# Retention and a mixture of experts on one core: where gating, weight splits and transposed rows stand in the engines' queues

## The chip, the cores and the metric

The kernel runs on one core of a Trainium2 chip. A core has five engines with a queue of instructions each: TensorE (PE; its weight loads are listed as PEld), VectorE (DVE), ScalarE (ACT), GpSimd (POOL) and SyncE (SP), which issues most of the transfers. Each queue is worked off in its order, and engines wait for one another by semaphores. The metric is the time of one execution on the device in microseconds (us), as the median of several.

## What is computed

Two steps stand one behind the other. The first is retention: attention without a softmax, causal, with a decay for each head. The second is a mixture of eight experts, in which each row goes to one expert.

```python
scores = scale * np.matmul(q, k.transpose(0, 1, 3, 2))     # q, k, v: 8 x 8 heads x 576 x 64
Dmat = np.where(rel >= 0, gamma[:, None, None] ** rel[None, :, :], 0.0)
x = np.matmul(scores * Dmat[None], v)                      # then as rows: x is 4608 x 512

logits = x @ w_gate                                        # 512 x 8
e_idx = np.argmax(logits, axis=1)
gate_w = softmax(logits)[np.arange(N), e_idx]
eom = 1.0 / (1.0 + np.exp(-(x @ w_output_gate)))
for e in range(E):                                         # 8 experts
    mask = e_idx == e
    h = np.maximum(x[mask] @ w1[e], 0.0)                   # 512 x 1024
    ye = h @ w2[e]                                         # 1024 x 512
    out[mask] = gate_w[mask, None] * eom[mask, e, None] * ye
```

Everything is float32. The host only rearranges arrays and adds tables of constants (decays, masks, row numbers).

## The kernel before

**Retention.** The 4608 rows are 36 tiles of 128. A loop over g = 0 ... 35 (L494) works them off with a running state for each head, so that a tile needs its own scores and the state before it. In the loop's code stand, in this order: `load` (the pack of tile g+4: q and k transposed, v as it is), `prep` (GpSimd scales v to vp), `scores(g+1)` (TensorE; VectorE masks them from PSUM into S_sb, two instructions), `k_rows(g+1)` (TensorE transposes k, ScalarE copies it to kn), `xnat(g-1)` (TensorE turns the finished tile xT back into rows and, in the same matmuls, forms the gating logits; ScalarE copies the rows to xgrp, VectorE copies the logits to lg in two instructions), `outT(g)` (TensorE applies state and scores; VectorE scales the result into xT), and `update(g)` (TensorE adds to the state; ScalarE copies it to stT). Nine tiles are two sequences of 576 rows: with c = g modulo 9, tile c = 8 updates no state, tile c = 0 reads none, and c = 4 holds the seam of two sequences.

Inside the blocks called `manual_schedule` the order of the code is the order of each engine's queue. So what is written ahead of `outT` stands ahead of xT on VectorE, and TensorE's `xnat` of the next round waits for that xT.

**Gating.** Every GT = 4 tiles, `gate1` (L371) finds the expert of each of 512 rows (13 small instructions on VectorE and two exponentials on ScalarE), `gate2` counts rows by matmuls with 0/1 matrices, `gate3a` and `gate3b` (VectorE) make the slot number and the weight of each row. Then `scatter_x` on GpSimd writes the rows into a table xs in device memory, 4608 slots for each expert; its calls lie in a list, `todo`, from which each tile takes one or two. After group 5 (tile 26) `gate3b` also makes the slots that are filled up with zeros.

**Experts.** Each expert has room for 616 rows here: part 0 with 360 rows (tiles t = 0, 1, 2) and part 1 with 256 (t = 3, 4); rows beyond that go through a loop at the end (L666). Each operand is split into an upper part, rounded to float32r, and a lower part, the difference; a product takes three matmuls (hi x hi, hi x lo, lo x hi). `mm1(e, part, fb)` makes one 128-row block of h in 12 matmuls into one of four PSUM buffers h_ps; ScalarE writes relu(h_ps) as hh (L244), VectorE the rest as hl (L245). `mm2(e, t)` makes a tile of y in 24 matmuls into one of two buffers y_ps; ScalarE scales it, GpSimd scatters it to the output (L264). For each expert the loop at L625 runs fb = 0 ... 7 with both parts, then t = 0 ... 4.

The weights come in eight pieces an expert (w1 and w2, four each, 512 KB a piece) through three staging buffers st: `start_w` issues the load, `hi_w` makes the upper half on ScalarE (L137, two instructions), `lo_w` the lower half on VectorE (L142, two instructions); `load_w` (L144) does all three with both halves on VectorE (L146, L147). The pieces of expert 0 are spread over the retention stage by the table `wsched`: for each piece the tiles at which load, `hi_w` and `lo_w` come. The rows of expert e+1 are loaded during the first half of expert e (`load_x`) and transposed during its second half by `transp` (L210): from expert 1 on VectorE transposes (L224), ScalarE casts the upper part xh (L226), VectorE subtracts to xl (L227). For expert 0 TensorE transposes (L221), at tiles 34 and 35.

Of the kernel before, what the change touches and what calls it, by code (L numbers as in the profile page):

```python
# [10 lines left out]
F32 = mybir.dt.float32  # L11
# [36 lines left out]
def tile_retention_moe(  # L48
# [95 lines left out]
    def load_w(which, e, fp):  # L144
        st, hi, lo = start_w(which, e, fp)
        V.tensor_copy(hi, st)  # L146
        V.tensor_tensor(out=lo, in0=st, in1=hi.bitcast(F32), op=ALU.subtract)  # L147

# [60 lines left out]

    def transp(e, t):  # L210
        part, n = (0, TA * P) if t < TA else (1, CAP - CA)
        t0 = t if part == 0 else t - TA
        if (e, part) not in XT:
            pl = pools[f"xt{part}"]
            XT[e, part] = (pl.tile([P, KB, n], F32R, name=f"xh{part}"), pl.tile([P, KB, n], F32R, name=f"xl{part}"))
        m = ROWS[t] if e == 0 else P
        hi, lo = (a[:, :, P * t0:P * t0 + m] for a in XT[e, part])
        if e == 0:
            src = pools["ps_x"].tile([P, KB, P], F32, name=pools["x_ps"])[:, :, 0:m]
            for k in range(KB):  # L220
                T.transpose(src[:, k, :], XG[e, t][0:m, k:DM:KB], ident[0:m, 0:m])  # L221
        else:
            src = pools["xq"].tile([P, KB, P], F32, name="x_t", bufs=2)
            V.transpose(out=src.rearrange("p k (u j) -> p u k j", u=4),  # L224
                        in_=XG[e, t].rearrange("p u (i k) -> p u k i", k=KB))
        A.copy(out=hi, in_=src)  # L226
        V.tensor_tensor(out=lo, in0=src, in1=hi.bitcast(F32), op=ALU.subtract)  # L227

# [141 lines left out]

    def gate1(n):  # L371
        L = gt["lg"]
# [11 lines left out]
        oh = sm.tile([P, GT, E], BF16, name="oh")  # L384
        V.tensor_tensor(out=oh, in0=fst, in1=bc(m2), op=ALU.is_equal)
        c1 = sm.tile([P, GT, E], BF16, name="c1")
        if n == 0:
# [83 lines left out]
    for n in (512, 512, 256):  # L471
        T.matmul(warm[:, 0:n], lhsT=zx[:, 0:P], rhs=zx[:, 0:n], start=True, stop=True)
    prep(0)

    wsched = {(1, 0): (6, 10, 11), (1, 1): (10, 14, 15), (1, 2): (15, 18, 19), (1, 3): (18, 22, 23),
              (2, 0): (25, 28, 29), (2, 1): (28, 31, 31), (2, 2): (30, 33, 33), (2, 3): (34, 36, 36)}
    wparts = {}
# [13 lines left out]
    with tc.manual_schedule():  # L491
        S_next = scores(0)
        k_rows(0)
        for g in range(NTILE):  # L494
# [12 lines left out]
            if g + 1 < NTILE:  # L507
                prep(g + 1)
                S_next = scores(g + 1)
                if "sl" in gt:  # L510
                    gate3b()
                k_rows(g + 1)
            for _ in range(1 if g < GT * SNAP + 6 else 2):
                if todo:
                    G.memset(gap, 0.0)
                    todo.pop(0)()
            if g >= NTILE - 2:
                transp(0, g - NTILE + 2)
            if g > 0:
                xnat(g - 1)  # L520
            outT(g, S_sb, prev)
            update(g)
            if g == NTILE - 1:
                transp(0, 2)
            if g % GT == 0 and g > 0:
                gate1(g // GT - 1)
            weights(g)
    psctx.close()
# [5 lines left out]
    xnat(NTILE - 1)  # L534
    gate1(NTILE // GT - 1)
    p1ctx.close()
# [88 lines left out]
    for e in range(E):  # L625
        nx = e + 1 < E
        for fb in range(FB):
# [14 lines left out]
            elif nx:  # L642
                if fb < CT:
                    load_x(e + 1, fb)
                if fb in (5, 6):
                    load_idx(e + 1, fb - 5)
                if fb % 2 == 1:
                    load_w(1, e + 1, fb // 2)
            if fb == (7 if e else 4) and e + 2 < E:
                fill_slots(e + 2)  # L650
        if e == E - 1:
            overflow_table()
        for t in range(CT):
            if e > 0 or t >= TA:
                for u in (t,) if e else range(3) if t == TA else range(3, CT):
                    if nx:
                        transp(e + 1, u)
                mm2(e, t)
# [98 lines left out]
```

## Time and profile before

| | |
|---|---|
| time, median of 3 | 637.74 us (635.58 to 639.58) |
| the profiled execution | 639.73 us, of which the span from first to last instruction is 637.9 us |
| VectorE busy | 353.1 us in 748 instructions |
| ScalarE busy | 173.3 us in 387 instructions |
| mean granted TensorE clock | 0.995 of full speed |
| stages in this profile | retention to about 182 us, expert 0 to about 240 us, then about 55 us for each further expert |

A row of a profile gives the line of the kernel, the engine, the operation and its tiles as out<-in. In a timeline two numbers stand ahead: the start from the span's beginning and the duration in us; "xN" is the number of instructions merged into the row, and in brackets stands how long the engine had been idle before it and what ended that. In a list of waits the three numbers are the total in us, how often, and the longest. Matmuls overlap, so that one lasts longer than the distance from its start to the next one's.

### The profile page before, as it was taken

The page shows a single profiled execution, that of the slowest core. Times are in us where ns is not written, and L with a number is a line of the kernel's source. Part 1 is how long each engine was busy: PE and PEld are TensorE (multiplying, and loading weights), DVE is VectorE, ACT ScalarE, POOL GpSimd, SP SyncE. Part 2 cuts the span into 40 slices and gives each one's busy share as a digit, 9 for nine tenths or more (in the row PEclk, how much of TensorE's full clock was granted, in tenths as well). Part 3 has the DMA queues.
Part 4 walks back from the last instruction along what each step waited for, and adds up shares of the span by engine and source line. Part 5 has one row for each costly group of instructions (what it writes and reads, how often), then busy time and mean ns, then how long its engine had stood idle before and what let it go on. Part 6 is the DMA issues. An engine that isn't in the chain of part 4 may idle for free. (4 is left out here: it accounts for less than half of the span.)

```text
span 637.9 us, 12795 instructions
## 1 busy us (share of the span) xinstructions
PE 620.4 (97%) x5135; PEld 550.1 (86%) x5135; DVE 353.1 (55%) x748; ACT 173.3 (27%) x387; POOL 166.0 (26%) x229
## 2 busy tenths in 40 slices
PE   8999999999989998999999999999999999999995
PEld 6888888888879888978997997898799789879974
DVE  4576887767743266751862475186257528625420
ACT  2333434333431333222222222222222122222210
POOL 2243445454227315012301401230150110010011
PEclk9999999999999998999999999999999999999999
DMA  9867697786314654741733364173345407311001
GB/s 323 250 237 264 221 313 231 240 278 216 115 69 163 185 157 140 200 126 53 211 91 109 101 195 132 41 205 91 113 129 167 132 31 221 110 47 49 0 34 43
DMA packets 54746, 96.24 MB, mean 151 GB/s; under 512 B 14640, under 2 KB 35505, under 8 KB 54684
## 3 DMA queue, kind: packets, MB, share of 16 engines
q1 hardware_dynamic: 44972, 72.99, 37.7%
q0 software_dynamic: 9280, 21.36, 9.2%
q8 instruction: 41, 0.67, 0.4%
q10 hardware_dynamic: 432, 1.05, 0.4%
q14 instruction: 21, 0.17, 0.1%
HBM read 74.02 MB, written 30.64 MB: 164 GB/s over the span
## 5 line engine op out<-in xcount | busy, mean ns | idle before, releaser
L240 PE MATMUL h_ps<-xh,w1h 128*128 128x360 f32 (+1 forms) x512 | 157.0, 307 | 6.0 <-ACT xh L226 3.9
L240 PE MATMUL h_ps<-xl,w1h 128*128 128x360 f32 (+1 forms) x512 | 156.7, 306 | 0.5 <-DVE xl L227 0.5
L240 PE MATMUL h_ps<-xh,w1l 128*128 128x360 f32 (+1 forms) x512 | 156.5, 306 | 0.0
L264 POOL DMA_INDIRECT out_dram<-y,idx x40 | 40.4, 1009 | 340.4 <-ACT y L263 312.6
L258 PE MATMUL y_ps<-w2h,hh 128*128 128x512 f32 (+1 forms) x320 | 125.8, 393 | 0.0
L258 PE MATMUL y_ps<-w2h,hl 128*128 128x512 f32 (+1 forms) x320 | 125.3, 391 | 0.0
L258 PE MATMUL y_ps<-w2l,hh 128*128 128x512 f32 (+1 forms) x320 | 125.2, 391 | 0.0
L245 DVE SCALAR_TENSOR_TENSOR hl<-h_ps,hh 128x360 fp32r<-128x360 f32 (+1 forms) x128 | 58.3, 474 | 98.1 <-ACT hh L244 92.6
L240 PEld LDWEIGHTS h_ps<-xh,w1h 128*128 128x128 f32 x512 | 97.4, 190 | 7.4 <-ACT xh L226 4.4
L240 PEld LDWEIGHTS h_ps<-xl,w1h 128*128 128x128 f32 x512 | 97.4, 190 | 1.7 <-DVE xl L227 1.0
L244 ACT ACTIVATE hh<-h_ps 128x360 fp32r<-128x360 f32 (+1 forms) x128 | 54.4, 428 | 160.6 <-PE h_ps L240 150.8
L240 PEld LDWEIGHTS h_ps<-xh,w1l 128*128 128x128 f32 x512 | 97.2, 190 | 0.0
L258 PEld LDWEIGHTS y_ps<-w2h,hl 128*128 128x128 f32 (+1 forms) x320 | 58.8, 184 | 15.0
L258 PEld LDWEIGHTS y_ps<-w2l,hh 128*128 128x128 f32 (+1 forms) x320 | 58.8, 184 | 14.2
L258 PEld LDWEIGHTS y_ps<-w2h,hh 128*128 128x128 f32 (+1 forms) x320 | 58.8, 184 | 14.2
L227 DVE TENSOR_TENSOR xl<-x_t,xh 128x512 fp32r<-128x512 f32 x35 | 24.2, 693 | 80.3 <-ACT xh L226 78.2
L263 ACT ACTIVATE y<-y_ps,idx 128x512 f32<-128x512 f32 (+1 forms) x40 | 27.5, 688 | 148.2 <-issue 77.2
L330 DVE TENSOR_TENSOR S_sb<-sc,cmat_sb 128x512 f32<-128x512 f32 x72 | 46.1, 682 | 17.8 <-PE sc L324 15.8
L313 POOL TENSOR_TENSOR vp<-pk,gk_sb 128x512 f32<-128x512 f32 x36 | 37.4, 1040 | 67.2 <-PE st_ps L344 44.3
L188 POOL DMA_INDIRECT xs<-xgrp,sli x36 | 37.1, 1031 | 49.8 <-issue 37.1
L188 POOL DMA_INDIRECT xs<-zx,fill x40 | 46.6, 1165 | 9.4 <-issue 9.4
L324 PE MATMUL sc<-pk 64*128 64x128 f32 x576 | 45.1, 288 | 0.8 <-DVE S_sb L330 0.4
(119 smaller groups left out, 676.0 us busy)
## 6 DMA issues: line engine op xcount, KB each, us to landing
st<-in_w_dram SPq DMA_DIRECT2D x64, 512.0 KB
pk<-in_pack_dram SPq DMA_DIRECT2D x32, 768.0 KB
x_q<-xs SPq DMA_DIRECT2D x140, 64.0 KB
gq_sb<-in_gq_dram SPq DMA_DIRECT2D x5, 256.0 KB
pk<-in_pack_dram SPq DMA_DIRECT2D x4, 256.0 KB
pk<-in_pack_dram SPq DMA_DIRECT2D x2, 512.0 KB
x_g<-xs SPq DMA_DIRECT2D x4, 256.0 KB
xs<-zx,fill POOLq DMA_INDIRECT x40
```

What stands on the lines that cost most here:

```text
L188: i = G.indirect_dma_start(out=xs, out_offset=bass.IndirectOffsetOnAxis(ap=at, axis=0), in_=x, in_offset=None, **({} if bound is None else ...
L227: V.tensor_tensor(out=lo, in0=src, in1=hi.bitcast(F32), op=ALU.subtract)
L240: i = T.matmul(ps, lhsT=a[:, k, :], rhs=b[:, k, 0:n], start=(j == 0), stop=(j == 3 * KB - 1))
L244: A.activation(out=hh, in_=ps, func=AF.Relu)
L245: V.scalar_tensor_tensor(out=hl, in0=ps, scalar=0.0, in1=hh.bitcast(F32), op0=ALU.max, op1=ALU.subtract)
L258: i = T.matmul(ps, lhsT=a[:, n], rhs=b, start=(j == 0), stop=(j == 3 * FB - 1))
L263: A.activation(out=y, in_=ps, func=AF.Copy, scale=idx.bitcast(F32)[0:m, e, t, 1:2])
L264: G.indirect_dma_start(out=out, out_offset=bass.IndirectOffsetOnAxis(ap=idx[0:m, e, t, 0:1], axis=0), in_=y, in_offset=None, bounds_check= ...
L313: G.tensor_tensor(out=vs[g], in0=pk[g][:, 2].rearrange("p (h d) -> p h d", h=H), in1=gk_sb[:, g % CPB].broadcast_to([P, H, D]), op=ALU.mult)
L324: T.matmul(sc[r][:, p], lhsT=k, rhs=q, start=True, stop=True)
L330: V.tensor_tensor(out=S_sb[:, r], in0=sc[r], in1=m, op=ALU.mult)
```

## The change

- `gate1` is cut in two: `gate1a` (six instructions, up to the one-hot choice oh) and `gate1b` (seven on VectorE and the two exponentials). They come at g % 4 = 0 and 1; `gate3b` at 2.
- In each tile, gating, `todo` and `weights(g)` now stand behind `xnat(g-1)` and ahead of `outT(g)`; before, `gate3b` stood ahead of `k_rows`, and `gate1` and `weights` behind `update`.
- `wsched`: seven of the eight pieces of expert 0 have load, `hi_w` and `lo_w` at g % 4 = 3, both halves in one tile (7, 11, ... 31); the eighth is unchanged.
- `load_w` makes the upper half by `hi_w` on ScalarE and the lower by `lo_w` on VectorE.
- From expert 1 on, the w1 pieces of the next expert come at fb = 5 and 7 and ahead of tiles t = 1 and 3 instead of at fb = 1, 3, 5 and 7.
- `transp` is cut in two, and the subtraction for tile u-1 stands behind the transposition and cast of tile u. For expert 1 all five tiles now stand ahead of `mm2(0, 3)`; before, three did, and two ahead of `mm2(0, 4)`.

```diff
--- before.py
+++ after.py
@@ -142,9 +142,9 @@
             V.tensor_tensor(out=lo[:, k], in0=st[:, k], in1=hi[:, k].bitcast(F32), op=ALU.subtract)
 
     def load_w(which, e, fp):
-        st, hi, lo = start_w(which, e, fp)
-        V.tensor_copy(hi, st)
-        V.tensor_tensor(out=lo, in0=st, in1=hi.bitcast(F32), op=ALU.subtract)
+        w = start_w(which, e, fp)
+        hi_w(*w)
+        lo_w(*w)
 
 
     XG, XT, HT = {}, {}, {}
@@ -208,6 +208,9 @@
         return [[partial(scatter_x, zx, i[:, e, j:j + 1], E * NT - 1) for j in range(nj)] for e in range(e1 - e0)]
 
     def transp(e, t):
+        transp_lo(*transp_hi(e, t))
+
+    def transp_hi(e, t):
         part, n = (0, TA * P) if t < TA else (1, CAP - CA)
         t0 = t if part == 0 else t - TA
         if (e, part) not in XT:
@@ -224,6 +227,9 @@
             V.transpose(out=src.rearrange("p k (u j) -> p u k j", u=4),
                         in_=XG[e, t].rearrange("p u (i k) -> p u k i", k=KB))
         A.copy(out=hi, in_=src)
+        return src, hi, lo
+
+    def transp_lo(src, hi, lo):
         V.tensor_tensor(out=lo, in0=src, in1=hi.bitcast(F32), op=ALU.subtract)
 
     def mm1(e, part, fb):
@@ -368,7 +374,7 @@
                         in1=gq_sb[:, :, c0:c0 + P].rearrange("p (r s) i -> p r s i", r=2), op=ALU.mult)
         xT[g] = x
 
-    def gate1(n):
+    def gate1a(n):
         L = gt["lg"]
         l, z = L[:, :, 0:8], L[:, :, 8:16]
         bc = lambda a: a.broadcast_to([P, GT, E])
@@ -383,6 +389,10 @@
         V.tensor_reduce(out=m2, in_=fst, op=ALU.max, axis=AX.X)
         oh = sm.tile([P, GT, E], BF16, name="oh")
         V.tensor_tensor(out=oh, in0=fst, in1=bc(m2), op=ALU.is_equal)
+        gt["half"] = (n, oh, lm, z)
+
+    def gate1b():
+        n, oh, lm, z = gt.pop("half")
         c1 = sm.tile([P, GT, E], BF16, name="c1")
         if n == 0:
             V.memset(c1[:, 0], 0.0)
@@ -472,8 +482,8 @@
         T.matmul(warm[:, 0:n], lhsT=zx[:, 0:P], rhs=zx[:, 0:n], start=True, stop=True)
     prep(0)
 
-    wsched = {(1, 0): (6, 10, 11), (1, 1): (10, 14, 15), (1, 2): (15, 18, 19), (1, 3): (18, 22, 23),
-              (2, 0): (25, 28, 29), (2, 1): (28, 31, 31), (2, 2): (30, 33, 33), (2, 3): (34, 36, 36)}
+    wsched = {(1, 0): (4, 7, 7), (1, 1): (7, 11, 11), (1, 2): (11, 15, 15), (1, 3): (15, 19, 19),
+              (2, 0): (19, 23, 23), (2, 1): (23, 27, 27), (2, 2): (27, 31, 31), (2, 3): (34, 36, 36)}
     wparts = {}
 
     def weights(g):
@@ -507,24 +517,27 @@
             if g + 1 < NTILE:
                 prep(g + 1)
                 S_next = scores(g + 1)
-                if "sl" in gt:
-                    gate3b()
                 k_rows(g + 1)
+            if g >= NTILE - 2:
+                transp(0, g - NTILE + 2)
+            if g > 0:
+                xnat(g - 1)
+
+            if g % GT == 0 and g > 0:
+                gate1a(g // GT - 1)
+            if "half" in gt and g % GT == 1:
+                gate1b()
+            if "sl" in gt:
+                gate3b()
             for _ in range(1 if g < GT * SNAP + 6 else 2):
                 if todo:
                     G.memset(gap, 0.0)
                     todo.pop(0)()
-            if g >= NTILE - 2:
-                transp(0, g - NTILE + 2)
-            if g > 0:
-                xnat(g - 1)
+            weights(g)
             outT(g, S_sb, prev)
             update(g)
             if g == NTILE - 1:
                 transp(0, 2)
-            if g % GT == 0 and g > 0:
-                gate1(g // GT - 1)
-            weights(g)
     psctx.close()
     ps_h = mctx.enter_context(tc.tile_pool(name="ps_h", bufs=4, space=PSUM, side="right", reuse_waits="tile"))
     pools["ps_h"] = ps_h
@@ -532,7 +545,8 @@
     rest.__enter__()
     mm1(0, 0, 0)
     xnat(NTILE - 1)
-    gate1(NTILE // GT - 1)
+    gate1a(NTILE // GT - 1)
+    gate1b()
     p1ctx.close()
     actx.close()
 
@@ -644,17 +658,25 @@
                     load_x(e + 1, fb)
                 if fb in (5, 6):
                     load_idx(e + 1, fb - 5)
-                if fb % 2 == 1:
-                    load_w(1, e + 1, fb // 2)
+                if fb in (5, 7):
+                    load_w(1, e + 1, (fb - 5) // 2)
             if fb == (7 if e else 4) and e + 2 < E:
                 fill_slots(e + 2)
         if e == E - 1:
             overflow_table()
+        xw = {}
         for t in range(CT):
             if e > 0 or t >= TA:
-                for u in (t,) if e else range(3) if t == TA else range(3, CT):
+
+                for u in range(CT) if e == 0 and t == TA else (t,) if e else ():
                     if nx:
-                        transp(e + 1, u)
+                        xw[u] = transp_hi(e + 1, u)
+                        if u > 0:
+                            transp_lo(*xw[u - 1])
+                        if u == CT - 1:
+                            transp_lo(*xw[u])
+                if e and nx and t in (1, 3):
+                    load_w(1, e + 1, 2 + t // 2)
                 mm2(e, t)
     mctx.close()
 
```

TensorE's queue is the same instruction by instruction. VectorE's, in the retention stage before, around the piece of weights at tile 11 and the gating at tile 12 (w1l is the lower half of a piece, mx to m the beginning of `gate1`):

```order
L366 TENSOR_TENSOR xT<-o_ps,gq_sb 128x512
L142 TENSOR_TENSOR w1l_637<-st,w1h_636 128x512 x2
L330 TENSOR_TENSOR S_sb<-sc_987,cmat_sb 128x512
L330 TENSOR_TENSOR S_sb<-sc_988,cmat_sb 128x512
L464 COPY lg<-xa 128x16
L465 TENSOR_TENSOR lg<-xb,lg 128x16
L366 TENSOR_TENSOR xT<-o_ps,gq_sb 128x512
L376 TENSOR_REDUCE mx<-lg 128x4
L378 TENSOR_TENSOR lm<-lg,mx 128x32
L380 TENSOR_TENSOR fst<-lg,mx 128x32
L381 TENSOR_TENSOR fst<-fst,csm_sb 128x32
L383 TENSOR_REDUCE m_1054<-fst 128x4
```

And after the change, at the same two tiles:

```order
L475 TENSOR_TENSOR lg<-xb,lg 128x16
L142 TENSOR_TENSOR w1l_674<-st,w1h_673 128x512 x2
L372 TENSOR_TENSOR xT<-o_ps,gq_sb 128x512
L336 TENSOR_TENSOR S_sb<-sc_995,cmat_sb 128x512
L336 TENSOR_TENSOR S_sb<-sc_996,cmat_sb 128x512
L474 COPY lg<-xa 128x16
L475 TENSOR_TENSOR lg<-xb,lg 128x16
L382 TENSOR_REDUCE mx<-lg 128x4
L384 TENSOR_TENSOR lm<-lg,mx 128x32
L386 TENSOR_TENSOR fst<-lg,mx 128x32
L387 TENSOR_TENSOR fst<-fst,csm_sb 128x32
L389 TENSOR_REDUCE m_1032<-fst 128x4
```

Both w1l and the gating have moved from behind xT to ahead of it; `oh` and then xT follow the last row, and the second half of gating stands in the next tile.

VectorE at the hand-over from expert 0 to expert 1 before (x_t is a transposed tile, xl its lower part):

```order
L224 STREAM_TRANSPOSE x_t<-x_q 128x4x4x32
L227 TENSOR_TENSOR xl_3371<-x_t,xh_3370 128x4x128
L224 STREAM_TRANSPOSE x_t<-x_q 128x4x4x32
L227 TENSOR_TENSOR xl_3371<-x_t,xh_3370 128x4x128
L224 STREAM_TRANSPOSE x_t<-x_q 128x4x4x32
L227 TENSOR_TENSOR xl_3371<-x_t,xh_3370 128x4x128
L224 STREAM_TRANSPOSE x_t<-x_q 128x4x4x32
L227 TENSOR_TENSOR xl_3415<-x_t,xh_3414 128x4x128
L224 STREAM_TRANSPOSE x_t<-x_q 128x4x4x32
L227 TENSOR_TENSOR xl_3415<-x_t,xh_3414 128x4x128
```

And after:

```order
L227 STREAM_TRANSPOSE x_t<-x_q 128x4x4x32 x2
L233 TENSOR_TENSOR xl_3371<-x_t,xh_3370 128x4x128
L227 STREAM_TRANSPOSE x_t<-x_q 128x4x4x32
L233 TENSOR_TENSOR xl_3371<-x_t,xh_3370 128x4x128
L227 STREAM_TRANSPOSE x_t<-x_q 128x4x4x32
L233 TENSOR_TENSOR xl_3371<-x_t,xh_3370 128x4x128
L227 STREAM_TRANSPOSE x_t<-x_q 128x4x4x32
L233 TENSOR_TENSOR xl_3384<-x_t,xh_3383 128x4x128 x2
```

Each subtraction now stands one transposition later.

VectorE in two blocks of expert 2 before (hl is the lower part of h, one row for each part of the expert's rows; w2h and w2l are the halves of a piece of w2):

```order
L245 SCALAR_TENSOR_TENSOR hl_4041<-h_ps,hh_4040 128x360
L245 SCALAR_TENSOR_TENSOR hl_4058<-h_ps,hh_4057 128x256
L146 CAST w2h_4076<-st 128x1024
L147 TENSOR_TENSOR w2l_4077<-st,w2h_4076 128x1024
L146 CAST w1h_4087<-st 128x1024
L147 TENSOR_TENSOR w1l_4088<-st,w1h_4087 128x1024
L245 SCALAR_TENSOR_TENSOR hl_4092<-h_ps,hh_4091 128x360
L245 SCALAR_TENSOR_TENSOR hl_4109<-h_ps,hh_4108 128x256
```

And after, ScalarE's queue in the first blocks of expert 1, to which the casts have gone:

```order
L250 ACTIVATE hh_3454<-h_ps 128x360
L250 ACTIVATE hh_3471<-h_ps 128x256
L137 CAST w2h_3490<-st 128x512 x2
L250 ACTIVATE hh_3501<-h_ps 128x360
L250 ACTIVATE hh_3518<-h_ps 128x256
L137 CAST w2h_3537<-st 128x512 x2
```

The cast of a piece stands between the blocks of hh on ScalarE; on VectorE only L142, in two instructions, stands behind the second hl of a block.

## Prediction

> **What bounds the kernel now.** I read the busy shares first, then the stretches, then who waited for whom on TensorE.
>
> ```profile
> PE 620.4 (97%) x5135; PEld 550.1 (86%) x5135; DVE 353.1 (55%) x748; ACT 173.3 (27%) x387; POOL 166.0 (26%) x229
> ```
>
> TensorE (PE) is busy nearly throughout; VectorE (DVE) has 45% of the span free, ScalarE (ACT) 73%. Work that only leaves those two engines is worth nothing by itself: an edit pays where TensorE waits. The next rows are stretches of the span: length, then busy time of PE, PEld, DVE, ACT and POOL, the granted TensorE clock, DMA share and GB/s.
>
> ```profile
> 16.00:128.00 112.00, 111.89 (x1768) 99.34 (x1764) 82.10 (x248) 41.05 (x110) 46.80 (x64) 1.00 0.75 252
> 128.00:182.00 54.00, 49.64 (x728) 42.72 (x724) 36.30 (x124) 20.16 (x52) 25.13 (x40) 1.00 0.59 197
> ...
> 240.00:256.00 16.00, 13.82 (x83) 13.21 (x82) 10.69 (x15) 4.48 (x10) 8.56 (x12) 0.89 0.44 133
> ...
> 366.00:490.00 124.00, 122.28 (x710) 110.52 (x709) 72.04 (x103) 29.09 (x59) 24.23 (x30) 1.00 0.47 138
> ```
>
> TensorE stands still for 4.36 us late in the retention stage (up to 182), for 2.18 us where expert 0 hands over to expert 1 (240 to 256), and for 1.72 us in experts 2 to 4. TensorE's waits name the engines:
>
> ```profile
> PE h_ps L240 <- ACT xh L226: 3.9, 2, 2.1
> PE h_ps L240 <- DVE hl L245: 1.7, 3, 1.1
> ...
> PE xb L454 <- DVE sl L417: 0.7, 2, 0.5
> PE xa L454 <- DVE xT L366: 0.6, 2, 0.3
> ```
>
> These are small, and a busy matmul can hide a stall, so I measure the retention stage by its pace: the starts of four tiles' scores (tiles 2, 8, 11 and 35).
>
> ```profile
> 12.11 0.38 PE L324 MATMUL sc<-pk 64*128 64x128 f32 x2
> ```
> ```profile
> 40.57 0.49 PE L324 MATMUL sc<-pk 64*128 64x128 f32 x4
> ```
> ```profile
> 53.36 0.48 PE L324 MATMUL sc<-pk 64*128 64x128 f32 x2
> ```
> ```profile
> 169.75 0.38 PE L324 MATMUL sc<-pk 64*128 64x128 f32 x2
> ```
>
> TensorE's work repeats every nine tiles. The first nine take 53.36 - 12.11 = 41.25 us, their first six 28.46. At that pace the 33 tiles from 2 to 35 need 3 x 41.25 + 28.46 = 152.21 us; they took 157.64. So 5.4 us is lost to late VectorE and ScalarE work, almost all behind tile 11.
>
> **The retention stage.** One tile, with the weight split where it stands now:
>
> ```profile
> 61.50 0.37 ACT L459 COPY xgrp<-xb 128x256 f32<-128x256 f32 x1
> 61.91 0.18 DVE L465 TENSOR_TENSOR lg<-xb,lg 128x16 f32<-128x16 f32 x1 [0.27 <-DVE lg L464]
> ...
> 63.14 0.69 DVE L366 TENSOR_TENSOR xT<-o_ps,gq_sb 128x512 f32<-128x512 f32 x1 [1.05 <-PE o_ps L362]
> ...
> 63.66 1.03 POOL L313 TENSOR_TENSOR vp<-pk,gk_sb 128x512 f32<-128x512 f32 x1 [1.67 <-PE st_ps L344]
> 63.74 2.10 DVE L142 TENSOR_TENSOR w1l<-st,w1h 128x512 fp32r<-128x512 f32 x2
> ...
> 65.07 0.66 PE L454 MATMUL xa<-iw,xT 128*128 128x144 f32 x4
> ```
>
> VectorE is idle 1.05 us ahead of xT, and xT ends 1.24 us before the matmul that reads it. In such a tile about 2.2 us fit between lg (ends at 62.09) and xT; before, gating and splits stood behind xT and pushed the next tile's S_sb, sl and lg. Now, piece by piece, with xT due at 65.07 less 0.13 us of signalling, so 64.94:
>
> ```profile
> 59.12 1.14 ACT L137 CAST w1h<-st 128x512 fp32r<-128x512 f32 x2
> ```
> ```profile
> 150.50 1.28 DVE L142 TENSOR_TENSOR w2l<-st,w2h 128x512 fp32r<-128x512 f32 x2
> ```
>
> Weight tiles (7, 11, ... 31): the upper halves follow xgrp on ScalarE at 61.87, the first ready at about 62.5, the second at 63.0; stT, queued behind them, only becomes possible at 63.66, so nobody waits for that. The lower halves run from 62.55 for 1.28 us to 63.85, and xT ends at 64.55: 0.4 us to spare. Two prices stand for the pair: 1.28, and 2.10 beside GpSimd's vp. I take 1.28, since vp starts only at 63.66. At 2.10 xT ends at 65.35, 0.4 us late, 7 x 0.4 = 2.8 us in all. Nothing but xT and the next S_sb is queued behind the pair on VectorE.
>
> [...]
>
> ```profile
> 165.83 0.18 DVE L376 TENSOR_REDUCE mx<-lg 128x4 f32<-128x32 f32 x1
> ...
> 168.01 0.19 DVE L396 TENSOR_REDUCE zs<-zo 128x4 f32<-128x32 f32 x1
> ```
> ```profile
> 131.72 0.18 DVE L425 TENSOR_TENSOR sl<-sl,oh 128x32 f32<-128x32 f32 x1
> ...
> 132.96 0.18 DVE L437 RECIPROCAL xgrp<-zs 128x4 f32<-128x4 f32 x1
> ...
> 134.15 0.16 DVE L446 TENSOR_TENSOR base<-base,bump 128x1 f32<-128x1 f32 x1
> ```
>
> All of gate1 takes 2.37 us; its halves (6 and 7 of 13 instructions) take about 1.1 and 1.3, and xT ends at 62.09 + 1.3 + 0.69 = 64.1. The eight instructions of gate3b take 1.42, xT ends at about 64.3. Both fit. GpSimd's scatter, moved behind them in the code, keeps its place in GpSimd's own queue; it starts about 0.8 us later in one tile of four, and the vp behind it is wanted a tile later. The exception is tile 26: gate3b with the fill's eight instructions takes 2.59 us, and that tile is 0.46 us shorter, as it updates no state; xT ends about 0.95 us late. Tile 27 reads no state, is 0.6 us shorter and carries a weight piece: 0.2 us late. These 1.2 us stay of the 5.4. Behind tile 35 the waits for sl and xT (0.5 us) shrink to perhaps 0.3. **Gain 4.4 us**, between 1.6 (the dearer price above) and 5.9 (nothing left).
>
> The wait ahead of the first expert matmul stays: tile 35's last transposition is where it was.
>
> ```profile
> 181.95 0.43 PE L240 MATMUL h_ps<-xh,w1h 128*128 128x360 f32 x1 [2.09 <-ACT xh L226]
> ```
>
> **Expert 0 to expert 1.** Five transpositions, casts and subtractions alternate on VectorE and ScalarE:
>
> ```profile
> 233.08 1.08 DVE L224 STREAM_TRANSPOSE x_t<-x_q 128x512 f32<-128x512 f32 x1
> ...
> 242.31 0.32 PE L240 MATMUL h_ps<-xh,w1l 128*128 128x360 f32 x1
> ...
> 242.68 1.08 DVE L224 STREAM_TRANSPOSE x_t<-x_q 128x512 f32<-128x512 f32 x1
> ...
> 243.80 0.62 ACT L226 CAST xh<-x_t 128x512 fp32r<-128x512 f32 x1 [1.76 <-DVE x_t L224]
> ...
> 244.45 0.69 DVE L227 TENSOR_TENSOR xl<-x_t,xh 128x512 fp32r<-128x512 f32 x1 [0.68 <-ACT xh L226]
> ```
> ```profile
> 245.42 0.28 PE L240 MATMUL h_ps<-xh,w1l 128*128 128x256 f32 x1
> ```
> ```profile
> 247.26 0.50 PE L240 MATMUL h_ps<-xh,w1h 128*128 128x360 f32 x1
> ```
>
> One round takes (242.68 - 233.08)/4 = 2.40 us, 0.7 of it VectorE's wait for the cast. With the subtraction of tile u behind the transposition of u+1, the last transposition ends after 5 x 1.08 + 3 x 0.69 = 7.47 us, at 240.55; the cast is done by 241.25, the last subtraction by 241.95. TensorE wants the cast at 242.31 + 0.16 = 242.47. So its wait goes: the third matmul, at 245.42 now, would start at about 242.71, **2.7 us**. The margin is 1.2 us for the cast; if the rows of x came later than that, it would come off the gain. y of tile (0,3) waits on ScalarE behind five casts; the next user of its PSUM buffer is 25 us away.
>
> After this wait the matmuls run at half pace: they start 0.30 us apart from 247.26 on, and the granted clock in 240 to 256 is 0.89, a loss of 16 x 0.11 = **1.7 us**. Bounds 0 (the clock drops anyway) to 1.7; I take 1.7, because it is full in every other stretch that I show.
>
> [...]
>
> **Experts 1 to 7.**
>
> ```profile
> 427.71 0.38 ACT L244 ACTIVATE hh<-h_ps 128x256 fp32r<-128x256 f32 x1 [0.96 <-PE h_ps L240]
> ...
> 428.92 0.69 DVE L146 CAST w1h<-st 128x1024 fp32r<-128x1024 f32 x1 [1.52 <-DMA st<-in_w_dram]
> 429.69 0.47 ACT L244 ACTIVATE hh<-h_ps 128x360 fp32r<-128x360 f32 x1 [1.60 <-PE h_ps L240]
> 429.72 1.22 DVE L147 TENSOR_TENSOR w1l<-st,w1h 128x1024 fp32r<-128x1024 f32 x1
> ```
>
> With two weight pieces in a block of 3.3 us, VectorE has 2 x (0.69 + 1.22) of splits on top of its hl, and TensorE waits for hl three times (1.7 us). Now 52 casts (0.69 each) leave VectorE, ScalarE gets 52 x 1.14 = 59 us, and no block has more than one piece. A cast fits into ScalarE's 1.60 us idle between two blocks; VectorE then has about 0.95 + 1.28 us a block. **Gain 1.7 us**; bounds 0 and 2.2.
>
> **The sum.** 4.4 + 2.7 + 1.7 + 1.7 = 10.5 us, from the profiled 639.73 to 629.2. The median before, 637.74, is 2.0 below its profile; the half clock may be absent from the other runs. I put the median at **628.4**.
>
> **The rivals.**
> 1. *VectorE's queue only changes place* (0.17). xT becomes the late piece in the retention stage: the split costs 2.10 and gating is slowed by GpSimd too. The retention gain falls to 0, leaving 6.1: about 633.6 by the profile, 632.5 as a median. For it: the slack is 0.4 us in seven tiles. Against it: GpSimd is idle there.
> 2. *The half clock stays* (0.07), now behind the wait at 181.95: 1.7 us less, about 630.
> 3. *The upper parts hold up ScalarE* (0.08), slower. A cast that waits for its weights now stands ahead of hh, where it stood on VectorE. With four h_ps buffers TensorE runs three groups ahead, some 3 x 1.65 us, less 0.9 for hh and hl: 4.1 us of cover. There are 40 such casts ahead of an hh; the other gains (8.8) are eaten when each wait is 4.3 us long. At 4.6 us the loss is 40 x 0.5 - 8.8 = +11: about 649. Against it: the longest such wait above was 1.52, and the loads are spread wider.
> 4. *The waits have other causes* (0.06): the tiles behind 11 are held up by something that the order on VectorE doesn't touch, and the pieces save 2 us: 636.
>
> My forecast has 0.62. Below 631.4 is faster by over 1%, which is about what a measurement of this kernel can tell: the forecast, rival 2 and a third of rival 1 give 0.74; slower 0.08; the rest, 0.18, within 1%. The range reaches from 625 (every stall gone) to 635 (rival 1 with the clock kept, and some of rival 4).
>
> **What would show it.** Tile 35's scores at 164 to 166 us instead of 169.75; no half pace behind 240; no wait for hl on TensorE; VectorE's idle ahead of xT gone in all but plain tiles. I am wrong if xa waits for xT in the tiles 7, 11, ... 31, or if ScalarE's casts wait on weights by more than 4 us.

## The result, and the profile after

| | before | after | after, second time |
|---|---|---|---|
| median, us (lowest to highest) | 638.04 (635.58 to 639.58) | 630.34 (630.11 to 630.84) | 630.55 (630.07 to 631.05) |
| ratio to before, with its 95% interval | | 0.9884 (0.9852 to 0.9916) | 0.9876 (0.9825 to 0.9928) |
| profiled execution, and its span | 639.73, 637.9 | 630.84, 628.7 | 630.07, 628.1 |
| tile 2's scores to tile 29's | 125.94 | 125.56 | 124.61 |
| tile 29's scores to tile 35's | 31.70 | 29.24 | 28.74 |
| tile 35's scores to the first expert matmul | 12.20 | 12.14 | 12.14 |
| expert 0 | 58.60 | 60.19 | 59.88 |
| expert 1 | 58.99 | 54.77 | 54.77 |
| experts 2 to 6 together | 276.47 | 273.87 | 273.87 |
| expert 7 and the end | 61.93 | 61.88 | 61.89 |

The kernel became 7.7 us faster; 628.4 was forecast. The lower rows are distances between starts in the timelines of the three profiles: of a tile's scores, and of each expert's first matmul in h_ps. (The second time has its own 638.21 for the kernel before.) The spans differ by 9.2 us. Of that 2.8 come from the retention stage between the tiles 2 and 35, 4.2 from expert 1 and 2.6 from the experts 2 to 6; expert 0 took 1.6 us longer. The remaining 1.1 us lies ahead of tile 2, where nothing was changed, and the second time it is not there.

The busy shares of the changed kernel, from the page:

```profile
PE 614.7 (98%) x5135; PEld 547.4 (87%) x5135; DVE 319.1 (51%) x748; ACT 226.2 (36%) x491; POOL 157.5 (25%) x229
```

ScalarE (ACT) has 104 instructions and 53 us more, VectorE is 34 us less busy, TensorE 6. The stretches with the same columns as before (busy of PE, PEld, DVE, ACT, POOL, granted clock, DMA share, GB/s):

```profile
128.00:182.00 54.00, 50.09 (x715) 43.83 (x712) 34.41 (x117) 18.63 (x47) 25.17 (x40) 0.97 0.52 181
...
240.00:256.00 16.00, 16.00 (x116) 16.00 (x115) 8.50 (x16) 7.96 (x18) 6.67 (x12) 1.00 0.58 161
...
366.00:490.00 124.00, 124.00 (x714) 111.93 (x713) 59.43 (x97) 46.99 (x95) 20.39 (x30) 1.00 0.41 125
```

From 240 us to its last matmul TensorE never stands still. But the clock, full at the end of the retention stage before, is now 0.97 there: the half pace has moved. Who TensorE waited for in the changed kernel:

```profile
PE h_ps L246 <- ACT xh L229: 3.0, 1, 3.0
...
PE xa L464 <- DVE xT L372: 0.7, 2, 0.5
```

The waits for hl are gone, and of two waits for xh one is left, which grew from 2.09 to 2.99 us. Tile 35's scores, at 169.75 us before:

```profile
165.85 0.71 PE L330 MATMUL sc<-pk 64*128 64x128 f32 x8
```

A weight tile of the changed kernel, to set beside the one in the prediction:

```profile
61.08 1.14 ACT L137 CAST w1h<-st 128x512 fp32r<-128x512 f32 x2
...
61.73 1.29 DVE L142 TENSOR_TENSOR w1l<-st,w1h 128x512 fp32r<-128x512 f32 x2 [0.34 <-ACT w1h L137]
62.95 0.68 DVE L372 TENSOR_TENSOR xT<-o_ps,gq_sb 128x512 f32<-128x512 f32 x1
...
62.97 1.03 POOL L319 TENSOR_TENSOR vp<-pk,gk_sb 128x512 f32<-128x512 f32 x1 [1.02 <-PE st_ps L350]
...
64.38 0.66 PE L464 MATMUL xa<-iw,xT 128*128 128x144 f32 x4
```

The pair takes 1.29 us, as forecast, since vp starts only when it is done, and xT ends 0.75 us ahead of xa. Nothing is late here.

### The profile page after: what moved, and what is told of

It is laid out like the page before. It is cut to its first block, busy times and chain, and to the rows that moved or that the text cites. A ratio compares the mean times of both kernels' runs of the same rounds, so it can differ in the third digit from the quotient of the medians.

```text
span 628.7 us, 12882 instructions
## 1 busy us (share of the span) xinstructions
PE 614.7 (98%) x5135; PEld 547.4 (87%) x5135; DVE 319.1 (51%) x748; ACT 226.2 (36%) x491; POOL 157.5 (25%) x229
## 3 DMA queue, kind: packets, MB, share of 16 engines
q10 hardware_dynamic: 432, 1.05, 0.4%
## 5 line engine op out<-in xcount | busy, mean ns | idle before, releaser
L251 DVE SCALAR_TENSOR_TENSOR hl<-h_ps,hh 128x360 fp32r<-128x360 f32 (+1 forms) x128 | 60.0, 476 | 139.9 <-ACT hh L250 129.0
L142 DVE TENSOR_TENSOR w1l<-st,w1h 128x512 fp32r<-128x512 f32 x64 | 41.4, 688 | 50.0 <-ACT w1h L137 48.8
L142 DVE TENSOR_TENSOR w2l<-st,w2h 128x512 fp32r<-128x512 f32 x64 | 41.4, 688 | 2.6 <-ACT w2h L137 0.7
L330 PE MATMUL sc<-pk 64*128 64x128 f32 x576 | 42.0, 285 | 0.6 <-DMA pk<-in_pack_dram 0.6
```

Of the source, the lines that this page charges most:

```text
L142: V.tensor_tensor(out=lo[:, k], in0=st[:, k], in1=hi[:, k].bitcast(F32), op=ALU.subtract)
L251: V.scalar_tensor_tensor(out=hl, in0=ps, scalar=0.0, in1=hh.bitcast(F32), op0=ALU.max, op1=ALU.subtract)
L330: T.matmul(sc[r][:, p], lhsT=k, rhs=q, start=True, stop=True)
```

## The experiments

They came in three sets. Each set has its own runs of the kernel before, with medians of 631.62, 638.21 and 635.18 us, so ratios are compared, and microseconds only within a set. Where profiles are set side by side, it is by distances between starts as in the table above. The runs of the first two sets are noted with chip 8, those of the third with chip 7, so this number doesn't tell apart the two sets that differ most: where an expectation speaks of a chip, read a set.

### The three parts alone (first set)

The retention part alone: the experts' code is as before.

```diff
-                if fb in (5, 7):
-                    load_w(1, e + 1, (fb - 5) // 2)
+                if fb % 2 == 1:
+                    load_w(1, e + 1, fb // 2)
...
+                for u in (t,) if e else range(3) if t == TA else range(3, CT):
...
+                        transp(e + 1, u)
```

> Only the edits of the retention stage (gating in halves, seven weight pieces one to a tile of four, all of it ahead of outT); the experts as before. By the prediction's sum tile 35's scores start at 165 to 167 us (169.75 before), the wait between the experts 0 and 1 and its half clock are there as before, and the time falls by about 4 us, to 633 to 634. By the rival that VectorE's queue only changes place, tile 35's scores stay at 168 us or later and the time within 2 us of before.

Measured 628.24 us (627.47 to 628.59), ratio 0.9945 (0.9929 to 0.9962): 3.4 us. From tile 2's scores to tile 35's it took 153.15 us, and from there to the first expert matmul 9.73. The next two variants, with the retention code of before in the same set, took 156.77 and 156.23, then 10.71 and 10.70: so 3.1 to 3.6 us went between the tiles 2 and 35, and 1.0 behind them. Expert 1, whose code is as before, still took 56.77.

The transpositions alone: `transp_hi` and `transp_lo` in the new order, everything else as before.

```diff
-                for u in (t,) if e else range(3) if t == TA else range(3, CT):
+                for u in range(CT) if e == 0 and t == TA else (t,) if e else ():
...
+                        xw[u] = transp_hi(e + 1, u)
+                        if u > 0:
+                            transp_lo(*xw[u - 1])
```

> Only the transpositions overlapped with the subtractions. By the prediction's sum TensorE's wait for the cast of expert 1's rows (2.0 us and 0.6 us at about 244) goes, and the half clock behind it too: 2.7 + 1.7 us, 633 to 634. If the half clock is not due to that wait, it stays somewhere within 10 us of there and the gain is 2.7 us or less, about 635.5.

Measured 630.12 us (629.07 to 632.7), ratio 0.9978 (0.9964 to 0.9992): 1.5 us. Expert 1 took 55.40 us. The saving is the wait alone: in this set no profile shows half pace behind the hand-over, so there was no second part to win.

The weights of the experts alone: `load_w` through `hi_w`, and w1 spread.

```diff
-        V.tensor_copy(hi, st)
-        V.tensor_tensor(out=lo, in0=st, in1=hi.bitcast(F32), op=ALU.subtract)
+        hi_w(*w)
+        lo_w(*w)
...
-                if fb % 2 == 1:
-                    load_w(1, e + 1, fb // 2)
+                if fb in (5, 7):
+                    load_w(1, e + 1, (fb - 5) // 2)
```

> Only the weights of the experts 1 to 7: upper halves by ScalarE and the w1 pieces spread over the blocks. By the prediction's sum TensorE's three waits for hl go, 1.7 to 2.2 us: 636. By the rival that the casts hold up ScalarE, TensorE waits for hh or hl more than before and the time rises above 640.

Measured 630.75 us (630.32 to 631.5), ratio 0.9986 (0.9974 to 0.9998): 0.9 us. The experts 2 to 6 took 54.77 us each, and no wait for hl is listed. Together the three parts make 5.8 us of 631.6, 0.9% against the 1.2% of the change where before took 638: what differs between the sets seems to be how much there was to lose.

### The wait ahead of the first expert (first and third set)

```diff
-            outT(g, S_sb, prev)
-            update(g)
             if g == NTILE - 1:
                 transp(0, 2)
+            outT(g, S_sb, prev)
+            update(g)
```

The last transposition for expert 0 stands ahead of tile 35's outT.

> The changed kernel with tile 35's last transposition for expert 0 written ahead of outT(35), so that 1.7 us of matmuls stand between it and the first expert matmul. If the wait of 3.0 us at 178 is the chain transposition, cast, subtraction with a late signal from TensorE, it shrinks to under 1 us, and the half clock behind it goes too (1.7 us): 626 to 627. If something else holds TensorE, ScalarE and VectorE there (the signals come late wherever they stand), the wait only moves, and the time stays at 629.5 or above.

Measured 624.22 us (624.11 to 624.33), ratio 0.9886 (0.9869 to 0.9902). The wait for xh is gone from TensorE's list, and the clock stays full until the last microseconds (1.00 in every stretch up to 615 us, 0.84 behind it). In this set that proves little: the retention part alone, with the transposition at its old place, had a wait of only 0.59 us there and no half clock behind it (1.00 from 172 to 256 us; last section). The test is the third set, where the signal is late:

> The changed kernel with tile 35's last transposition for expert 0 ahead of the last outT, beside a new measurement of the kernel before. Where the kernel before took 631.6 us this variant took 624.2 (0.9886). Where the kernel before takes about 638 and the changed one 630.4, the theory (the wait of 3.0 us ahead of the first expert matmul brings the half clock behind it) expects both to go: 3.0 + 1.7 us less than 630.4, some 625.7, ratio 0.981, and no half clock ahead of the end. Rival: the half clock there does not come from this wait; then 627.4 with a half clock still somewhere near 178 us.

Measured 625.96 us (625.22 to 626.58), ratio 0.9851 (0.9819 to 0.9883). The time is the expected one; the ratio isn't, because the kernel before took 635.2 here and not 638. In the same set the variant with the casts on VectorE (below), which differs from the changed kernel only in who casts, took 629.71, with a wait of 2.9 us at this place and 6.8 us of half pace behind it. The stretches of the early transposition, then of the kernel with the casts on VectorE:

```profile
172.00:240.00 68.00, 67.31 (x420) 60.58 (x421) 31.84 (x78) 23.50 (x51) 25.75 (x39) 1.00 0.51 156
```
```profile
176.00:183.00 7.00, 6.26 (x22) 5.92 (x23) 1.90 (x4) 1.40 (x4) 0.00 (x0) 0.52 0.07 28
```

Where the wait is taken away, the half pace doesn't come: the rival that it stems from somewhere else near 178 us falls. The granted clocks of the runs agree, 0.997 to 0.998 here against 0.990 to 0.994 in the neighbour's. This variant is the fastest of all, 3.7 us below its neighbour in the set.

### The changed kernel and the kernel before, once more (second set)

No edit.

> The changed kernel once more, beside variants of it. On the first chip it took 630.34 us against 638.04 (ratio 0.988). On the chip of the last four runs the kernel before took only 631.6 us, and there the three parts alone saved 3.4, 1.5 and 0.9 us. If the parts add up and the first chip's extra stalls were the chip's own (GpSimd-independent: late signals at 175 and 221 us, the half clock), this run takes about 626 us on such a chip, with the wait ahead of the first expert matmul near 2.0 us and no half clock behind it. If the wait of 3.0 us and the half clock belong to the changed kernel, both are seen again, whatever the chip: some 628 to 630 us.

Measured 630.55 us (630.07 to 631.05), ratio 0.9876 (0.9825 to 0.9928). The wait is 2.99 us again, and the stretch behind it is the same as in the first profile:

```profile
178.00:181.00 3.00, 3.00 (x10) 2.68 (x10) 0.27 (x1) 0.00 (x0) 0.00 (x0) 0.50 0.00 1
```

In this set the kernel before takes 638 as at first, so it doesn't tell what the changed kernel would take where before takes 631.6.

> The kernel before, with a profile from the chip of these runs. Theory: what the hand-over from expert 0 to 1 and the wait ahead of the first expert matmul cost depends on the chip; if signals come without the lag of 1.5 to 3.9 us that the first chip shows behind 179 and 223 us, tile 35's last transposition is followed by its cast within 0.1 us, the wait ahead of the first expert matmul is below 2.09 us, and there is no half clock behind 247 us. Rival: the lag belongs to the kernel, and cast, wait (2.09 us) and half clock are as in the first profile.

One run, 635.65 us, beside a median of 638.21. Neither theory: the waits for xh are 2.05 ahead of the first expert and 0.9 at the hand-over, the clock in 240 to 256 us is full (1.00), and expert 1 takes 56.52 us where the first profile shows 58.99. The lag at the first place is that of the first profile (1.5 us from the transposition's end to its cast in both), so it is no accident of one run. The half pace at the second place comes in some runs and not in others. The granted clock of a run shows it: 0.995 in the first profile, 0.998 in this one. Of the 19 runs of before in this set, 14 are at 0.995 or less, and the two at 0.998 are the fastest (634.75 and 635.24 us), so most seem to have it.

### A weight piece behind the state update (second and third set)

```diff
-            weights(g)
             outT(g, S_sb, prev)
             update(g)
+            weights(g)
```

> The changed kernel with the pieces of weights put back behind the state update, at the same tiles (g % 4 = 3, where no gating is). Two theories on the retention gain. A: what paid is that gating and pieces no longer meet in one tile and that gating left the place behind xT; then a piece behind xT costs little more than the same piece ahead of it, since 2.10 us for the pair beside vp still end before the next tile's gating would start: within 0.5 us of the changed kernel. B: what paid is the idle slot ahead of xT, and a pair behind xT pushes the next tile's S_sb, lg and xT: with 2.10 - 1.28 = 0.8 us or less lost in each of 7 tiles, 2 to 3 us slower, xa waiting for xT in tiles 8, 12, ... 32.

Measured 638.46 us (636.71 to 638.93), ratio 1.0000 (0.9976 to 1.0024): the whole gain is gone, 7.9 us. Both theories were too small. The distance from tile 2's scores to tile 29's is 128.60 us (124.61 with the pieces ahead of xT), and from there to tile 35's 32.14 (28.74). A gating tile that follows a weight tile:

```profile
68.85 1.03 POOL L319 TENSOR_TENSOR vp<-pk,gk_sb 128x512 f32<-128x512 f32 x1 [2.25 <-PE st_ps L350]
68.91 1.03 DVE L391 TENSOR_TENSOR oh<-fst,m 128x32 bf16<-128x32 f32 x1
...
69.86 0.68 DVE L372 TENSOR_TENSOR xT<-o_ps,gq_sb 128x512 f32<-128x512 f32 x1
...
70.69 0.73 PE L464 MATMUL xa<-iw,xT 128*128 128x144 f32 x4 [0.26 <-DVE xT L372]
```

Against the changed kernel, and counted from the tile's scores, the pair behind xT has pushed S_sb by 1.1 us and the gating by 0.6. Its last instruction, oh, then meets vp on GpSimd and takes 1.03 us instead of 0.19; xT behind it is late, and TensorE waits.

In the second form the pieces stand behind the update too, but at the tiles 6, 10, ... 30, so that the tile after has no gating.

```diff
-    wsched = {(1, 0): (4, 7, 7), (1, 1): (7, 11, 11), (1, 2): (11, 15, 15), (1, 3): (15, 19, 19),
-              (2, 0): (19, 23, 23), (2, 1): (23, 27, 27), (2, 2): (27, 31, 31), (2, 3): (34, 36, 36)}
+    wsched = {(1, 0): (4, 6, 6), (1, 1): (6, 10, 10), (1, 2): (10, 14, 14), (1, 3): (14, 18, 18),
+              (2, 0): (18, 22, 22), (2, 1): (22, 26, 26), (2, 2): (26, 30, 30), (2, 3): (34, 36, 36)}
```

> The pieces of weights behind the state update as in the variant that lost 7.9 us, but one tile earlier (tiles 6, 10, ... 30), so that no gating stands in the next tile. Theory: what was lost there came from the gating, which the late piece pushed under GpSimd's vp; with no gating behind it a pair behind xT (about 1.3 us) only moves the next S_sb and lg by 0.4 us, and xT waits for TensorE anyway: within 1 us of the changed kernel. Rival: the idle slot ahead of xT is itself what pays; then 6 to 8 us slower again, with xa waiting for xT.

Measured 633.20 us (632.39 to 633.99), ratio 0.9958 (0.9937 to 0.9980), 3.5 us above the kernel with the casts on VectorE in the same set. It lies between the two expectations: the gating behind the piece makes about half of the loss, and the other half is the place itself:

```profile
60.64 2.83 DVE L142 TENSOR_TENSOR w1l<-st,w1h 128x512 fp32r<-128x512 f32 x2 [0.64 <-ACT w1h L137]
...
61.25 1.05 POOL L319 TENSOR_TENSOR vp<-pk,gk_sb 128x512 f32<-128x512 f32 x1
```

I had counted 1.3 us for the pair. Behind xT it met vp in this tile as well, and took 2.83; S_sb comes 3.79 us behind its scores instead of 1.19, and the next scores wait for it.

### Gating in one piece (second and third set)

```diff
-            if "half" in gt and g % GT == 1:
                 gate1b()
```

`gate1b` follows `gate1a` at once, at g % 4 = 0, ahead of xT.

> The changed kernel with the gating of a group in one piece again, at g % 4 = 0, ahead of xT. By the prediction's working xT ends at 62.09 + 2.37 + 0.69 = 65.15 us in tile 12 against 64.94 due: 0.2 us late in each of 8 tiles, 1.7 us slower than the changed kernel. Rival: the cut in halves is worth nothing, because the next matmuls' own slack takes 0.2 us up: within 0.5 us. A third: GpSimd's vp (1.03 us) now runs beside the second half of the gating and stretches it to 3 us or more; then 5 us slower or worse.

Measured 638.93 us (638.57 to 639.48), ratio 1.0008 (0.9984 to 1.0032): the third expectation, 8.4 us. In a gating tile:

```profile
69.76 1.29 DVE L402 TENSOR_TENSOR c<-c,oh 128x8 bf16<-128x8 bf16 x3
...
70.00 1.03 POOL L319 TENSOR_TENSOR vp<-pk,gk_sb 128x512 f32<-128x512 f32 x1 [2.51 <-PE st_ps L350]
```

Three additions of eight numbers a row take 1.29 us beside vp. To see whether vp is the cause, and not only near, the vp that would meet the gating was then made by ScalarE, in this same kernel:

```diff
+    def prep_act(g, h0):
+        for h in range(h0, h0 + H // 2):
+            A.activation(out=vs[g][:, h], in_=pk[g][:, 2, D * h:D * h + D], func=AF.Copy, scale=gk_sb[:, g % CPB, h])
...
+        if g >= 6 and g % GT == 2:
+            prep_act(g, 0)
+            return
```

> The variant with gating in one piece (638.9 us, 8.4 slower than the changed kernel), in which the one vp that would run beside the second part of the gating (the rows of tiles 6, 10, ... 34) is made by ScalarE in eight copies instead of by GpSimd. Theory: GpSimd's vp holds VectorE's instructions with two operands in SBUF until it ends (oh and c took 1.0 to 1.3 us there against 0.2 and 0.5), and that is all that the cut in halves avoids beyond 0.2 us a tile. Then no instruction of the gating takes over 0.6 us, xT is about 0.2 us late in each of 8 tiles, and the time comes to 2 us above the changed kernel: some 632 to 633 where the kernel before takes 638. Rival: the gating is simply too long for the place ahead of xT, whoever makes vp: 637 to 639.

Measured 634.83 us (631.79 to 636.48), ratio 0.9987 (0.9966 to 1.0009). The groups by line between 60 and 140 us, gating in one piece with vp on GpSimd, then with vp on ScalarE (count, busy and mean ns of one):

```profile
L402 DVE TENSOR_TENSOR c<-c,oh 128x8 bf16<-128x8 bf16 x12 | 4.9, 408 | 0.4
```
```profile
L409 DVE TENSOR_TENSOR c<-c,oh 128x8 bf16<-128x8 bf16 x12 | 2.0, 163 | 0.4
```

The same twelve instructions take 163 ns each once GpSimd leaves them alone, and 408 beside it. From tile 2's scores to tile 29's, over six gatings, the first took 131.54 us, 6.9 more than the changed kernel, or 1.15 a gating; the second 126.97, 2.4 more, or 0.4 a gating, where 0.2 was expected. So vp is the cause of two thirds of the loss there. The rest fits the shortness of the place, but that is not shown: ScalarE's eight copies are new as well. Behind tile 29 this kernel lost another 4.2 us, with a stretch of half pace at 147 us, which I have not explained; the time as a whole is 5.1 us above the kernel with the casts on VectorE in the same set, where the theory allowed 2. Its ten runs are of two kinds, five at a granted clock of 0.996 to 0.998 with 631.8 to 634.3 us, and five at 0.993 with 635.4 to 636.5; the profile is one of the latter.

### The casts on VectorE again (third set)

```diff
-        hi_w(*w)
-        lo_w(*w)
+        V.tensor_copy(hi, st)
+        V.tensor_tensor(out=lo, in0=st, in1=hi.bitcast(F32), op=ALU.subtract)
```

> The changed kernel with the upper halves of the weights of experts 1 to 7 made by VectorE again; the spread of the w1 pieces stays. If two pieces in one block made TensorE wait for hl (VectorE's 2 x 1.91 us of splits beside 0.95 of hl in a block of 3.3), one piece a block leaves room (2.9 of 3.3 us) and nothing is lost: within 0.5 us of the changed kernel, no wait for hl. Rival: the casts on VectorE, which also wait there for the weights to land, are what made hl late; then the waits for hl (0.6 to 1.7 us in the two profiles of before) come back and the kernel is 1 to 2 us slower.

Measured 629.71 us (629.27 to 630.31), ratio 0.9905 (0.9873 to 0.9937). No wait for hl is listed, and each of the experts 1 to 6 takes 54.77 us as in the changed kernel. So in the experts the spread of the w1 pieces is enough by itself (ScalarE's casts without the spread were not run); that ScalarE makes the upper halves takes 27 us off VectorE (346.7 to 319.4 busy) and gives ScalarE 52, and TensorE waited for neither.

## Why the prediction was right, and where not

**Retention, 4.4 us: right.** In the first profile 2.8 us went between the tiles 2 and 35, in the second 4.3, in the part alone 3.1 to 3.6 of a smaller loss. The difference of the first two lies mostly in one wait at the beginning, for a table to land, which the second profile doesn't have. It takes back the 1.1 us gained ahead of tile 2: counted from the span's start, tile 35's scores come 3.9 us sooner than before. The wait in the first profile:

```profile
17.42 0.69 DVE L372 TENSOR_TENSOR xT<-o_ps,gq_sb 128x512 f32<-128x512 f32 x1 [3.03 <-DMA gq_sb<-in_gq_dram]
```

The weight tiles fit with room to spare. Behind tile 35, where I had given 0.2, the first set gained 1.0, and this pair nothing, since a late signal (last section) sets the end there. Of what should stay late, tile 26 did:

```profile
133.14 0.69 DVE L372 TENSOR_TENSOR xT<-o_ps,gq_sb 128x512 f32<-128x512 f32 x1
...
133.98 0.73 PE L464 MATMUL xa<-iw,xT 128*128 128x144 f32 x4 [0.46 <-DVE xT L372]
```

I had worked out 0.95 us; it is 0.46 of waiting, and xa starts 0.15 us behind the end of xT, where I had put 0.13 for the signal. For tile 27, where I had 0.2, no wait is listed. I had not seen tile 32, where the first half of the gating just touches vp:

```profile
160.78 1.04 POOL L319 TENSOR_TENSOR vp<-pk,gk_sb 128x512 f32<-128x512 f32 x1 [2.23 <-PE st_ps L350]
160.84 1.04 DVE L391 TENSOR_TENSOR oh<-fst,m 128x32 bf16<-128x32 f32 x1
```

The reason was right as well, but I gave it too small a place. The prediction let vp slow the weight pair only, 2.10 us beside it against 1.28, and put gating at its quiet durations; that GpSimd might slow it stands only in rival 1, set aside because "GpSimd is idle there". In the changed kernel it is, but for tile 32, and by little: oh ends 0.35 us before vp starts in tile 12. The experiments show that vp holds up gating too: oh takes 1.03 us beside it against 0.19, c 408 ns against 163. Either edit undone, some 8 us are lost (7.9 and 8.4), so rival 1 (VectorE's queue only changes place, 632.5) was nearer than its 0.17 says: 0.6 us later in its tile the gating meets vp.

**The hand-over, 2.7 us: right.** The last cast for expert 1 starts at 237.89 us and takes 0.62; TensorE, which began expert 1 at 238.18, never waits. The transpositions alone saved 1.5 us in a set in which that wait was shorter.

**The half clock, 1.7 us: the step that failed.** Behind the hand-over it is gone, and expert 1 is 4.2 us shorter, as 2.7 + 1.7 said. But I took it as gone altogether "because it is full in every other stretch", and rival 2 (0.07) came instead: it lies behind the first expert matmul now.

```profile
177.37 0.69 DVE L372 TENSOR_TENSOR xT<-o_ps,gq_sb 128x512 f32<-128x512 f32 x1 [4.04 <-remote]
177.43 0.51 ACT L229 CAST xh<-k_ps 128x416 fp32r<-128x416 f32 x1 [4.31 <-remote]
...
177.99 0.43 PE L246 MATMUL h_ps<-xh,w1h 128*128 128x360 f32 x1 [2.99 <-ACT xh L229]
```
```profile
179.00:182.00 3.00, 3.00 (x11) 3.00 (x11) 0.00 (x0) 0.00 (x0) 0.00 (x0) 0.50 0.00 0
```

Expert 0 took 1.6 us longer for it. That "the wait stays" was right in kind, but it grew by 0.9 us, and a stall of 2.99 us isn't one of 2.09: behind that one the clock was full (1.00 from 182 to 240 us). The stretch at half clock lasts 3.41 us in both first profiles (from 245.77 us before, from 178.67 after), and about twice that in two of the variants. With the 1.7 us for the half clock left out, my sum gives 630.9 for a profile that took 630.84; I put the median another 0.8 below, and it is at 630.34. That the sum without it meets the profile so closely is luck: in this pair 1.6 us of the 4.4 are missing between the tiles 2 and 35, while 1.1 us came ahead of tile 2 and 0.9 more than the 1.7 from the experts 2 to 6. That the half clock moved seems to hang in part on chance too: on where the wait falls between the times at which the clock can be seen to change (last section).

**The waits for hl, 1.7 us: right, low in this pair of profiles.** The experts 2 to 6 are 2.6 us shorter than in the first profile of before. In the second profile of before they take 274.92, only 1.05 above the changed kernel, and in the first set 0.9 was to be had. I named two causes, two pieces in a block and VectorE's casts; taking away the first is enough.

**Rivals 3 and 4.** ScalarE's casts hold up nobody: no wait for hh is listed. That the tiles wait for something else than VectorE's order was contradicted by the retention part alone, 153.15 us from tile 2 to tile 35 against a quiet pace of 152.21.

## What to carry to other kernels

A small instruction is short only while nothing holds it (here 163 ns alone and 408 beside vp): look up, for each place to which VectorE's work is to be moved, whether an instruction of GpSimd's like vp runs at that time, and take the duration beside it from the trace. Two edits that each look like an extra safety (cut in halves, moved ahead) can both be needed, so undo them one at a time before calling either superfluous. And when one of two stalls that can bring half clock is removed, price the half clock behind the other: here it made expert 0 longer by 1.6 us.

## What the hardware did that was not expected

**A signal that comes late.** In the changed kernel the recorded transposition ahead of the first expert ends at 175.00 us, but ScalarE starts its cast at 177.43, 2.4 us later; xT, released by TensorE just before, is as late. In the kernel before it was 1.5 us. With the retention part alone, in the first set, the cast follows at once:

```profile
173.84 0.73 PE L224 MATMUL k_ps<-cmat_sb,x_g 104*128 104x104 f32 x4
...
174.60 0.51 ACT L229 CAST xh<-k_ps 128x416 fp32r<-128x416 f32 x1 [1.91 <-PE k_ps L224]
...
175.16 0.43 PE L246 MATMUL h_ps<-xh,w1h 128*128 128x360 f32 x1 [0.59 <-ACT xh L229]
```

The lag goes with the set and with the place in the program, not with the transposition. All four profiles of the first set are prompt: three wait 0.59 to 0.60 us at this place, and the early transposition not at all. The others with the transposition at this place are late and wait 2.05 to 3.0 us. With the early transposition in the third set TensorE waits for no cast there either, but xT, at the old place, still starts 2.1 us behind its last matmul (174.19 to 176.31), where nobody waits for it. In six of these profiles, the prompt one with the retention part alone among them, a packet of instructions (0.02 MB) is fetched in the same 4 or 5 us, so the fetch alone doesn't explain it. What does is open.

It is also part of why the kernel before takes 631.6 us in one set and 638.2 in another: from tile 35's scores to the first expert matmul it is 12.2 us in both profiles of before, and 10.7 in the two profiles of the first set with this code. Another part is half clock: the granted clock of before is 0.996 to 0.999 in the first set and 0.991 to 0.998 in the second. The rest is open.

**How long a stall it takes.** In these profiles the waits ahead of the first expert of 2.9 and 3.0 us were each followed by 3.4 or 6.8 us at half clock, those of 0.59, 2.05 and 2.09 us by none. At the hand-over of the kernel before, one of 1.84 us had been enough. So the length of the one wait does not decide. In the first profiles of the two kernels the granted clock changes only at whole multiples of 3.4133 us from its first rise to full: before, counted from 6.84 us, at 70, 71 and 184 of them (245.77, 249.19 and 634.89); after, counted from 4.59, at 51, 52 and 182 (178.67, 182.08 and 625.81). Cut into steps of this length, these two profiles have half clock behind the steps in which TensorE was idle for 2.18 us, for 2.93 and, at the end, for all 3.41. Behind every other step, with up to 1.22 us of idle time, the clock is full. That is not the whole story: in the variant with vp on ScalarE, four waits between 144.4 and 147.0 us make 1.18 us, and the clock behind them is 0.57 in the mean from 147 to 151 us.

The wait of 2.09 us in the kernel before stands across the border of two steps, at 180.92, and leaves 1.06 and 1.22 us of idle time in them. The 1.84 us at the hand-over, with 0.34 more, lie inside one, 242.36 to 245.77, and make 2.18. The 2.99 us of the changed kernel put 2.93 into one. In two of the variants TensorE was idle for another 0.74 us (casts on VectorE, 176 to 183 us) and 0.85 us (pieces behind the update, 184 to 191) in a stretch whose clock was 0.52 and 0.51; there the half clock lasted about 6.8 us (the means make it 6.7 and 6.9). So a shift of the kernel by a microsecond may be enough to bring the half clock or take it away; no run here tests that alone.
